# Values of an attention in four parts of the array, in two turns with two banks

## The chip, the cores and the metric

One core of a Trainium2 chip. The time is the device's microseconds for one execution of the whole program. The engines are TensorE (PE, its weight loads listed apart as PEld), VectorE (DVE), ScalarE (ACT), GpSimd (POOL) and SyncE (SP, which issues the loads). PE writes its results to PSUM, which has eight banks of 128 partitions x 512 floats.

## The reference

A sliding-window attention with sink tokens, and two feed-forward networks behind it, all in float32:

```python
# q, k, v: (2, 8, 768, 64), n_sink 4, window 128
scores = q @ k^T / 8
keep = (key < n_sink) | ((0 <= query - key) & (query - key < window))
a = softmax(where(keep, scores, -1e9))
x = (a @ v), heads side by side                # 1536 tokens x 512
x = ((x @ w_a) * (x @ w_b)) @ w_out            # d_ff 1536
out = square(max(x @ w_in, 0)) @ w_out2        # d_ff 2048
```

## The kernel before

The attention goes over 24 groups g of 128 queries and four heads: batch b = g // 12, block i of 128 tokens = (g % 12) // 2, half m of the heads. A query block sees its own block of keys, the block before it (for i > 0), and eight sink tokens. A group goes through these stages:

- `scores`: two pairs of heads pp, each with a PSUM tile of two banks, `scs[pp]`. Each matmul multiplies 64 rows (one head's 64 features, `half(keys, r)`) with 64 queries, so four of them use the four parts of the array: r picks the rows, z the columns. A float32 matmul is two records of the trace (L233). For i > 0 they are 200 or 208 columns wide, else 128.
- `soft0`, `soft1` (`maxima`, DVE L249 and L252): selection, mask and maximum, a pair at a time; `exp0`, `exp1` (ACT L260); `rec` (DVE L265, L266): sum and reciprocal.
- `sp` (POOL L289 to L291): the sinks' weights; `pst`, `st`: their transposition on PE (L321) and its copy by ACT (L327). `norm`, `normA`, `normP`: normalizing on DVE, ACT (L275) and POOL.
- `ptp` (PE L297): transposes the four heads' weights into one bank; `th` (ACT L301) copies that out; `lu` (POOL L312, L314) makes two masked copies, `lu[:, 0]` for the block itself (a key sees later queries) and `lu[:, 1]` for the block before (a key sees earlier queries).
- `x` (`values`, PE L335, L340): for each block j and head, a matmul of 128 keys x 64 features with 128 queries, two heads beside each other in the two column halves of the array; then two matmuls for the sinks, into the same bank. `xh` (ACT L348) and `xl` (DVE L351) split it into a rounded part and the rest.

Beside this runs `Beside`: `fill` issues the twelve matmuls (L660) of a piece of the first network's product into a bank of `psa`; `fu` (ACT L673) or `fm` (DVE L677) drains it in the next step. A fill may start when 512 tokens are attended: steps 11 to 26 have one each. `abs`, `ts`, `stt`, `stt2`, `cast`, `lo` decode weights (ACT L533, L549, DVE L537 to L551). `warm` issues small matmuls in the steps 0 to 4.

The order of the work on PE, DVE, ACT and POOL is written by hand: for each step g, `ORDER` names the stages in turn with a lag, so ("x", -3) is the x of group g - 3. Each engine takes its own instructions in that order; a wait on one stops all behind it. SP issues its loads by itself.

PSUM: four banks of scores; `bank()` hands out the rest in rotation for ptp, pst, x and warm, four banks until step 10 and two from then on, when two go to `psa`. Code that the change touches:

Of the kernel before, what the change touches and what calls it, by code (L numbers as in the profile page):

```python
# [10 lines left out]
F32 = mybir.dt.float32  # L11
# [19 lines left out]
    ("exp0", -1), ("exp1", -1), ("fm", 0), ("pst", -2), ("rec", -1), ("st", -2), ("fu", 0), ("scores", 0),  # L31
    ("x", -3), ("abs", 0), ("xh", -3), ("ptp", -2), ("th", -2), ("cast", -2), ("soft0", 0), ("soft1", 0), ("sp", -1),
# [3 lines left out]
WIDE = 10  # L36
# [113 lines left out]
def attention_fast(tc, ctx, c, cp, tp, q, k, v, vs_in, xh, xl, beside):  # L150
# [11 lines left out]
    banks = [ctx.enter_context(tc.tile_pool(name="ps_t", bufs=2, space=PSUM))]  # L162
    wide = ctx.enter_context(ExitStack())
    banks.append(wide.enter_context(tc.tile_pool(name="ps_u", bufs=2, space=PSUM, side="right")))
    turn = [0]

    def bank(name):

        turn[0] += 1
        return banks[turn[0] % len(banks)].tile([P, GH, P], F32, name=name, tag="tr")  # L170
# [49 lines left out]
    def scores(g):  # L220

        b, i, m = groups[g]
        n = b * NB + i
        for pp, sc in enumerate(scs):
            for r in range(2):
                row = half(keys, r)[:, 2 * m + pp].rearrange("d n s -> d (n s)")
                for z in range(2):
                    at, u0, u1 = PREV, i * SW, i * SW + P
                    if i > 0 and z == 0:
                        u0, u1 = u0 - SW, u0 + HK  # L230
                    elif i > 0:
                        at, u0, u1 = 0, u0 - PREV, u0 + SW
                    nc.tensor.matmul(sc[z * HK:(z + 1) * HK, r, at:at + u1 - u0],  # L233
                                     lhsT=half(queries[n], r)[:, 2 * m + pp, z * HK:(z + 1) * HK], rhs=row[:, u0:u1],
                                     start=True, stop=True)
# [93 lines left out]
    def values(g):  # L329

        b, i, m = groups[g]
        x = xs[g] = bank("x")[:, 0:2]
        for j, probs_t in enumerate(lus.pop(g)):
            for h in range(GH):
                nc.tensor.matmul(half(x, h % 2)[:, h // 2], lhsT=vals[g // 2 - j][:, GH * m + h], rhs=probs_t[:, h],  # L335
                                 start=j == 0 and h < 2, stop=False, skip_group_check=True)
        if i > 0:
            st = sts.pop(g)
            for pp in range(2):
                nc.tensor.matmul(x[:, pp], lhsT=vs[:, b, 2 * m + pp, :], rhs=st, start=False, stop=False,  # L340
                                 skip_group_check=True)
# [14 lines left out]
    def warm(n):  # L356
# [4 lines left out]
        for _ in range(n):  # L361
# [3 lines left out]
    stages = dict(scores=scores, ptp=probs, th=probs_copy, lu=probs_select, soft0=lambda g: maxima(g, 0),  # L365
                  soft1=lambda g: maxima(g, 1), exp0=lambda g: exps(g, 0), exp1=lambda g: exps(g, 1), rec=reciprocal,
                  sp=sinks, pst=sinks_turn, st=sinks_copy, x=values, xh=x_high, xl=x_low,
                  norm=normalize, normA=normalize_a, normP=normalize_p)
    warm(WARM0)
    for g in range(N + 3):  # L370
        if g == WIDE:
            banks.pop()
            wide.close()
            beside.open()
# [223 lines left out]
class Beside:  # L598
# [12 lines left out]
    def open(self):  # L611
        self.ps = self.stack.enter_context(self.tc.tile_pool(name="ps_a0", bufs=2, space=PSUM, side="right"))
# [29 lines left out]
class Ffn:  # L642
# [9 lines left out]
    def inner(self, ph, f, j, ts, ps_a):  # L652
# [3 lines left out]
        ps = ps_a.tile([P, ts.stop - ts.start], F32, name="psa", tag="z", bufs=2)  # L656
# [7 lines left out]
    def ahead(self, t0, last, beside, wk):  # L664
# [4 lines left out]
        for f in range(AHEAD1):  # L669
            u = wk.tile([P, T], F32, name="u", tag="u")  # L670
            pa = self.inner(0, f, 0, ts, beside.ps)
# [3 lines left out]
            pb = self.inner(0, f, 1, ts, beside.ps)  # L675
# [396 lines left out]
def sliding_window_moe_kernel(ctx, tc, q, k, v, vs, span, w_a, w_b, w_out, w_in2, w_out2, out):  # L1072
# [19 lines left out]
    def run(attend):  # L1092
# [3 lines left out]
        with ExitStack() as c0:  # L1096
# [3 lines left out]
            with ExitStack() as c1, tc.manual_schedule(engines=ORDERED):  # L1100
                attend(c1, beside)
            with tc.tile_pool(name="sb", bufs=1) as sb, tc.tile_pool(name="ks", bufs=NKEEP) as keep:
# [21 lines left out]
    def attend_any(ctx, beside):  # L1124
        attention_any(tc, c, q, k, v, xh, xl)
        beside.open()
# [74 lines left out]
```

## Time and profile before

| | |
|---|---|
| median of 3 runs | 627.29 us (625.4, 627.29, 627.45) |
| the profiled execution | 625.55 us, span 623.8 us |
| PE busy | 610.1 us, 98% of the span, 3302 matmul records |
| PEld, DVE, ACT, POOL busy | 79%, 77%, 50%, 9% |
| first fill | 46.97 us |
| x of the last group | 123.88 us |

The busy time of PE counts overlapping records once, and its ends are modelled. Times in the rows are us from the start of the span. A row of the order of time merges like instructions that follow each other (x16); in brackets stands how long the engine was idle before, and what released it.

### The profile page before, as it was taken

The numbers are of one execution on the slowest core, as the hardware profiler recorded it, in microseconds if no ns is written. First come the engines' busy times: TensorE is split into PE (matmuls) and PEld (weight loads), VectorE is DVE, ScalarE is ACT, GpSimd is POOL, SyncE is SP. The second block draws the span as 40 slices with busy tenths as digits, with TensorE's granted clock in tenths as the row PEclk, the third lists the DMA queues.
The fourth block names the chain that finished last, engine by engine and source line by source line (L and its number), as shares of the span: only waits on it lengthen the run. The fifth ranks groups of instructions, "written<-read, shape, count | busy, mean of one in ns | idle before, by whom it ended". The sixth has DMA issues, their size and how long they took to land.

```text
span 623.8 us, 9222 instructions
## 1 busy us (share of the span) xinstructions
PE 610.1 (98%) x3302; PEld 494.0 (79%) x3302; DVE 483.2 (77%) x1099; ACT 309.2 (50%) x706; POOL 56.5 (9%) x132
## 2 busy tenths in 40 slices
PE   9789999999999999999999999999999999999996
PEld 5557777888888888888888888888888888888884
DVE  7999998369999848959769999976797679834352
ACT  6998887525754424534433554563454345332220
POOL 2564255400000000000000000000000000000000
PEclk9999999999999999999999999999999999999999
DMA  8844423001223412202212013132032202000023
GB/s 273 260 117 151 153 69 102 2 34 55 82 92 112 126 43 101 69 34 68 101 35 101 1 34 102 69 108 95 34 102 68 68 34 68 0 2 2 0 100 108
DMA packets 22039, 49.51 MB, mean 79 GB/s; under 512 B 2080, under 2 KB 8736, under 8 KB 21984
## 3 DMA queue, kind: packets, MB, share of 16 engines
q1 hardware_dynamic: 21696, 48.70, 24.0%
q8 instruction: 28, 0.46, 0.3%
q14 instruction: 27, 0.22, 0.1%
q10 hardware_dynamic: 288, 0.13, 0.1%
HBM read 45.68 MB, written 3.15 MB: 78 GB/s over the span
## 4 chain that ended last, share of the span: by engine, by line


## 5 line engine op out<-in xcount | busy, mean ns | idle before, releaser
L660 PE MATMUL psa<-xh,wh 128*128 128x512 f32 x224 | 88.7, 396 | 0.0
L660 PE MATMUL psa<-xh,wl 128*128 128x512 f32 x224 | 87.5, 391 | 0.0
L660 PE MATMUL psa<-xl,wh 128*128 128x512 f32 x224 | 87.3, 390 | 0.0
L920 PE MATMUL acc<-wh,gh 128*128 128x512 f32 x192 | 74.8, 389 | 0.0
L920 PE MATMUL acc<-wh,gl 128*128 128x512 f32 x192 | 74.8, 389 | 0.0
L920 PE MATMUL acc<-wl,gh 128*128 128x512 f32 x192 | 74.7, 389 | 0.0
L551 DVE TENSOR_TENSOR wl<-wtmp,wh 128x512 fp32r<-128x512 f32 x68 | 47.3, 700 | 17.3 <-ACT wh L549 17.0
L549 ACT CAST wh<-wtmp 128x512 fp32r<-128x512 f32 x68 | 42.3, 622 | 37.0 <-PE acc L920 10.1
L67 ACT CAST gh<-ks 128x512 fp32r<-128x512 f32 x48 | 29.6, 621 | 52.5 <-PE acc L920 52.5
L533 ACT ACTIVATE wtmp<-wraw 128x512 f32<-128x512 f32 x68 | 45.7, 676 | 19.4 <-DVE wl L68 12.7
L920 PE MATMUL acc<-gl,wh 128*128 128x512 f32 x136 | 52.9, 389 | 0.0
L920 PE MATMUL acc<-gh,wl 128*128 128x512 f32 x136 | 52.9, 389 | 0.0
L920 PE MATMUL acc<-gh,wh 128*128 128x512 f32 x136 | 52.9, 389 | 0.0
L660 PEld LDWEIGHTS psa<-xh,wl 128*128 128x128 f32 x224 | 42.1, 188 | 9.0
L660 PEld LDWEIGHTS psa<-xl,wh 128*128 128x128 f32 x224 | 42.1, 188 | 8.3
L660 PEld LDWEIGHTS psa<-xh,wh 128*128 128x128 f32 x224 | 42.1, 188 | 8.2
L541 DVE SCALAR_TENSOR_TENSOR wtmp<-wraw,wtmp 128x512 int32<-128x512 int32 x68 | 47.0, 694 | 0.4
L544 DVE SCALAR_TENSOR_TENSOR wtmp<-wraw,wtmp 128x512 int32<-128x512 int32 x68 | 46.3, 684 | 0.7
L920 PEld LDWEIGHTS acc<-wh,gh 128*128 128x128 f32 x192 | 36.0, 188 | 7.5
L920 PEld LDWEIGHTS acc<-wh,gl 128*128 128x128 f32 x192 | 36.0, 188 | 7.5
L920 PEld LDWEIGHTS acc<-wl,gh 128*128 128x128 f32 x192 | 36.1, 188 | 7.4
L68 DVE TENSOR_TENSOR gl<-ks,gh 128x512 fp32r<-128x512 f32 x48 | 32.7, 686 | 10.3 <-ACT gh L67 9.9
(170 smaller groups left out, 1274.9 us busy)
## 6 DMA issues: line engine op xcount, KB each, us to landing
wraw<-in_moe_w_out_dram SPq DMA_DIRECT2D x28, 512.0 KB, 3.5
wraw<-in_moe_w_in_dram SPq DMA_DIRECT2D x16, 512.0 KB, 3.5
wraw<-in_moe_w_a_dram SPq DMA_DIRECT2D x12, 512.0 KB, 3.5
wraw<-in_moe_w_b_dram SPq DMA_DIRECT2D x12, 512.0 KB, 3.5
values<-in_v_dram SPq DMA_DIRECT2D x12, 256.0 KB, 4.3
keys<-in_k_dram SPq DMA_DIRECT2D x11, 272.0 KB, 4.8
queries<-in_q_dram SPq DMA_DIRECT2D x11, 256.0 KB, 3.8
out_dram<-part SPq DMA_DIRECT2D x11, 256.0 KB, 2.2
```

The source lines that it names most:

```text
L67: nc.scalar.copy(hi, src)
L68: return (lo_eng or nc.vector).tensor_sub(lo, src, hi.bitcast(F32))
L533: a = nc.scalar.activation(tf, up.bitcast(F32), AF.Abs)
L541: nc.vector.scalar_tensor_tensor(out=t, in0=up, scalar=0x3FFFFFFF, in1=t, op0=ALU.bitwise_or, op1=ALU.bitwise_and)
L544: nc.vector.scalar_tensor_tensor(out=t, in0=low, scalar=29, in1=t, op0=ALU.logical_shift_right, op1=ALU.bitwise_or)
L549: nc.scalar.copy(hi, tf)
L551: nc.vector.tensor_sub(lo, tf, hi.bitcast(F32))
L660: self.tc.nc.tensor.matmul(ps, lhsT=w[:, kt, :], rhs=x[:, kt, ts], start=n == 0, stop=n == 3 * KT - 1)
L920: nc.tensor.matmul(acc["ps"][d], lhsT=a, rhs=b, start=n == 0, stop=n == acc["total"] - 1)
```

## The change

The values run in four parts of the array as well: the keys of a block are cut into upper and lower 64 rows (r), and the two column halves stay for the two heads of a pair. [...] Where a half of the keys can only see half of the queries, the matmul has 64 columns instead of 128 (`part`). In the order, scores are cut into the two pairs, and it goes scores0, x0, scores1, x1, xs (the sinks' product).

The banks: four for scores, two for x with one buffer, one for ptp, pst and warm together, and one for the fills from the start; when the attention is over, the fills get two others.

```diff
--- before.py
+++ after.py
@@ -28,12 +28,11 @@
 NRAW, AHEAD = 3, 2
 
 ORDER = [
-    ("exp0", -1), ("exp1", -1), ("fm", 0), ("pst", -2), ("rec", -1), ("st", -2), ("fu", 0), ("scores", 0),
-    ("x", -3), ("abs", 0), ("xh", -3), ("ptp", -2), ("th", -2), ("cast", -2), ("soft0", 0), ("soft1", 0), ("sp", -1),
+    ("exp0", -1), ("exp1", -1), ("fm", 0), ("pst", -2), ("rec", -1), ("st", -2), ("fu", 0), ("scores0", 0),
+    ("x0", -3), ("scores1", 0), ("x1", -3), ("xs", -3), ("abs", 0), ("xh", -3), ("ptp", -2), ("th", -2), ("cast", -2), ("soft0", 0), ("soft1", 0), ("sp", -1),
     ("norm", -1), ("warm", 0), ("fill", 0), ("normA", -1), ("normP", -1), ("xl", -3), ("stt", -1),
     ("lo", -2), ("ts", 0), ("lu", -2), ("stt2", -1)]
 DECODE = [4, 8, 10, 11, 12, 13, 14, 15, 18, 19, 20]
-WIDE = 10
 VS = (3, 6)
 PINNED = 3
 WARM0 = 14
@@ -159,15 +158,12 @@
     p1 = ctx.enter_context(tc.tile_pool(name="at1", bufs=1))
     p2 = ctx.enter_context(tc.tile_pool(name="at2", bufs=2))
     ps_s = ctx.enter_context(tc.tile_pool(name="ps_s", bufs=1, space=PSUM))
-    banks = [ctx.enter_context(tc.tile_pool(name="ps_t", bufs=2, space=PSUM))]
-    wide = ctx.enter_context(ExitStack())
-    banks.append(wide.enter_context(tc.tile_pool(name="ps_u", bufs=2, space=PSUM, side="right")))
-    turn = [0]
+    ps_t = ctx.enter_context(tc.tile_pool(name="ps_t", bufs=1, space=PSUM))
+    ps_x = ctx.enter_context(tc.tile_pool(name="ps_x", bufs=1, space=PSUM))
+    beside.open(1)
 
     def bank(name):
-
-        turn[0] += 1
-        return banks[turn[0] % len(banks)].tile([P, GH, P], F32, name=name, tag="tr")
+        return ps_t.tile([P, GH, P], F32, name=name, tag="tr")
 
     pns, ths, sps, sts, lus, xs = ({} for _ in range(6))
 
@@ -217,11 +213,11 @@
     for sc in scs:
         nc.vector.memset(sc[:, :, 0:PREV + SW + HK], 0.0)
 
-    def scores(g):
+    def scores(g, pp):
 
         b, i, m = groups[g]
         n = b * NB + i
-        for pp, sc in enumerate(scs):
+        for sc in scs[pp:pp + 1]:
             for r in range(2):
                 row = half(keys, r)[:, 2 * m + pp].rearrange("d n s -> d (n s)")
                 for z in range(2):
@@ -326,18 +322,40 @@
         sts[g] = p2.tile([96, P], F32R, name="st", tag="st", bufs=NSP)
         nc.scalar.copy(sts[g], sps.pop((g, "t")))
 
-    def values(g):
+    mark = p1.tile([1, 1], F32, name="mark")
+    marks = []
+
+    def behind(later, earlier):
+        tc.add_manual_dep(later.ins, earlier.ins.name, mybir.DependencyInfo(
+            mybir.DependencyClass.Sync, mybir.DependencyReason.DATA), reason="rows change places")
+
+    def values(g, turn):
 
         b, i, m = groups[g]
-        x = xs[g] = bank("x")[:, 0:2]
-        for j, probs_t in enumerate(lus.pop(g)):
-            for h in range(GH):
-                nc.tensor.matmul(half(x, h % 2)[:, h // 2], lhsT=vals[g // 2 - j][:, GH * m + h], rhs=probs_t[:, h],
-                                 start=j == 0 and h < 2, stop=False, skip_group_check=True)
+        if turn == 0:
+            xs[g] = ps_x.tile([P, 2, 512], F32, name="x", tag="x")[:, :, 0:P]
+        x, lu = xs[g], lus[g]
+        part = {(0, 0): slice(0, P), (0, 1): slice(0, HK), (1, 0): slice(HK, P), (1, 1): slice(0, P)}
+        for n in range(len(lu)):
+            for r in range(2):
+                j, pp = (n ^ r if i > 0 else n), r ^ turn
+                for h in range(2 * pp, 2 * pp + 2):
+                    mm = nc.tensor.matmul(half(x, h % 2)[:, pp, part[r, j]], lhsT=half(vals[g // 2 - j], r)[:, GH * m + h],
+                                          rhs=half(lu[j], r)[:, h, part[r, j]], start=n == 0 and turn == 0, stop=False,
+                                          skip_group_check=True)
+                    if turn == 1 and n == 0:
+                        behind(mm, marks[0])
+        if turn == 0:
+            marks[:] = [nc.gpsimd.memset(mark, 0.0)]
+            behind(marks[0], mm)
+
+    def sinks_values(g):
+        b, i, m = groups[g]
+        lus.pop(g)
         if i > 0:
             st = sts.pop(g)
             for pp in range(2):
-                nc.tensor.matmul(x[:, pp], lhsT=vs[:, b, 2 * m + pp, :], rhs=st, start=False, stop=False,
+                nc.tensor.matmul(xs[g][:, pp], lhsT=vs[:, b, 2 * m + pp, :], rhs=st, start=False, stop=False,
                                  skip_group_check=True)
 
     def places(g):
@@ -362,16 +380,12 @@
             nc.tensor.matmul(ps, lhsT=beside.zero, rhs=beside.zero[:, 0:1].to_broadcast([P, 2 * P]), start=True,
                              stop=True)
 
-    stages = dict(scores=scores, ptp=probs, th=probs_copy, lu=probs_select, soft0=lambda g: maxima(g, 0),
+    stages = dict(scores0=lambda g: scores(g, 0), scores1=lambda g: scores(g, 1), ptp=probs, th=probs_copy, lu=probs_select, soft0=lambda g: maxima(g, 0),
                   soft1=lambda g: maxima(g, 1), exp0=lambda g: exps(g, 0), exp1=lambda g: exps(g, 1), rec=reciprocal,
-                  sp=sinks, pst=sinks_turn, st=sinks_copy, x=values, xh=x_high, xl=x_low,
+                  sp=sinks, pst=sinks_turn, st=sinks_copy, x0=lambda g: values(g, 0), x1=lambda g: values(g, 1), xs=sinks_values, xh=x_high, xl=x_low,
                   norm=normalize, normA=normalize_a, normP=normalize_p)
     warm(WARM0)
     for g in range(N + 3):
-        if g == WIDE:
-            banks.pop()
-            wide.close()
-            beside.open()
         if g % 2 == 0:
             load_kq(g // 2 + 2)
             load_v(g // 2 + 1)
@@ -608,8 +622,9 @@
         self.open_piece = None
         self.work = self.head()
 
-    def open(self):
-        self.ps = self.stack.enter_context(self.tc.tile_pool(name="ps_a0", bufs=2, space=PSUM, side="right"))
+    def open(self, n):
+        self.ps = self.stack.enter_context(self.tc.tile_pool(name=f"ps_a{n}", bufs=n, space=PSUM, side="right"))
+        self.tags = n
 
     def head(self):
         for t0 in range(0, self.NT, T):
@@ -649,11 +664,11 @@
         self.chores = []
         self.pace = 1
 
-    def inner(self, ph, f, j, ts, ps_a):
+    def inner(self, ph, f, j, ts, ps_a, bufs=2):
         W, xh, xl = self.W, self.xh, self.xl
         KT = xh.shape[1]
         hi, lo = (w.rearrange("p (k f) -> p k f", k=KT) for w in W.get(ph, f, j))
-        ps = ps_a.tile([P, ts.stop - ts.start], F32, name="psa", tag="z", bufs=2)
+        ps = ps_a.tile([P, ts.stop - ts.start], F32, name="psa", tag="z", bufs=bufs)
         n = 0
         for kt in range(KT):
             for w, x in ((hi, xh), (hi, xl), (lo, xh)):
@@ -668,11 +683,11 @@
         ts = slice(t0, t0 + T)
         for f in range(AHEAD1):
             u = wk.tile([P, T], F32, name="u", tag="u")
-            pa = self.inner(0, f, 0, ts, beside.ps)
+            pa = self.inner(0, f, 0, ts, beside.ps, beside.tags)
             yield "fu"
             nc.scalar.copy(u, pa)
             yield None
-            pb = self.inner(0, f, 1, ts, beside.ps)
+            pb = self.inner(0, f, 1, ts, beside.ps, beside.tags)
             yield "fm"
             nc.vector.tensor_mul(self.gs[t0 // T][:, f], u, pb)
             if last:
@@ -1099,6 +1114,7 @@
             beside = Beside(tc, W, F, wk0, c0, zero, NT)
             with ExitStack() as c1, tc.manual_schedule(engines=ORDERED):
                 attend(c1, beside)
+            beside.open(2)
             with tc.tile_pool(name="sb", bufs=1) as sb, tc.tile_pool(name="ks", bufs=NKEEP) as keep:
                 sx = slots(sb, NSUM)
                 F.sx = {(n, k): sx[3 * k + n - 2] for n in range(2, 5) for k in range(2)}
@@ -1123,7 +1139,6 @@
 
     def attend_any(ctx, beside):
         attention_any(tc, c, q, k, v, xh, xl)
-        beside.open()
 
     run(lambda ctx, beside: attention_fast(tc, ctx, c, cp, tp, q, k, v, vs, xh, xl, beside))
     slow = nc.values_load(c.slow[0:1, 0:1], min_val=0, max_val=1,
```

## Rows read from the trace of the kernel before

**Rows 1.** busy time by stretch: us, then busy us (records) of each engine, clock, DMA

```profile
30.00:40.00 10.00, 7.74 (x91) 4.60 (x89) 8.74 (x44) 8.80 (x33) 6.72 (x17) 1.00 0.49 130
...
50.00:60.00 10.00, 10.00 (x101) 8.14 (x101) 9.86 (x35) 8.25 (x27) 5.07 (x9) 1.00 0.44 132
```

**Rows 2.** order of time, PE alone, second regime: start, us, line, operation

```profile
49.98 0.67 PE L233 MATMUL sc<-keys,queries 64*64 64x128 f32 x16
50.58 1.09 PE L335 MATMUL x<-lu,values 128*64 128x128 f32 x16
...
60.49 0.93 PE L233 MATMUL sc<-keys,queries 64*64 64x200 f32 x16
61.35 1.09 PE L335 MATMUL x<-lu,values 128*64 128x128 f32 x16
62.38 0.44 PE L340 MATMUL x<-st,vs 96*128 96x128 f32 x2
```

**Rows 3.** instructions of tile x: duration ns min/median/max, first and last start

```profile
L335 PE MATMUL x<-lu,values x320: 272/273/325, 20.3 to 124.7; 128*64 128x128 f32 x160
```

**Rows 4.** busy time of PE in one very short stretch, records in flight in brackets

```profile
27.34:27.37 0.03, 0.03 (x5) 1.00 0.33 137
```

**Rows 5.** order of time: a small POOL memset, and POOL's answer to ACT

```profile
0.30 0.10 POOL L1141 MEMSET const-float32-0.0<- 128x1 f32 x1 [0.30 <-issue]
...
35.01 0.58 ACT L301 COPY th<-ptp 128x512 f32<-128x512 f32 x1
...
35.67 0.64 POOL L312 TENSOR_SCALAR_AFFINE_SELECT lu<-th 128x512 f32<-128x512 f32 x1 [0.36 <-ACT th L301]
```

**Rows 6.** order of time, all engines, around step 7 (first regime)

```profile
25.86 0.18 DVE L266 RECIPROCAL ss<-ss 128x4 f32<-128x4 f32 x1
...
26.22 0.24 POOL L289 TENSOR_TENSOR ex<-ex,ss 128x32 f32<-128x32 f32 x1 [1.74 <-PE ptp L297]
...
26.84 0.25 POOL L291 TENSOR_TENSOR sp<-ex,sp 128x32 fp32r<-128x32 f32 x1
...
27.15 0.27 PE L321 MATMUL pst<-identr,sp 128*96 128x128 f32 x1 [1.09 <-POOL sp L291]
...
28.23 0.63 POOL L314 TENSOR_SCALAR_AFFINE_SELECT lu<-th 128x512 f32<-128x512 f32 x1
...
28.27 0.41 DVE L351 TENSOR_TENSOR xl<-x,xh 128x256 fp32r<-128x256 f32 x1
...
28.51 1.09 PE L335 MATMUL x<-lu,values 128*64 128x128 f32 x16
...
29.53 0.44 PE L340 MATMUL x<-st,vs 96*128 96x128 f32 x2
...
30.01 0.37 ACT L348 CAST xh<-x 128x256 fp32r<-128x256 f32 x1
...
30.52 0.58 ACT L301 COPY th<-ptp 128x512 f32<-128x512 f32 x1
```

**Rows 7.** order of time: last exponential on ACT and DVE's sum, two steps

```profile
33.07 0.19 ACT L260 ACTIVATION_READ_ACCUMULATOR ex<-ex,nb 128x1 f32 x1
...
33.30 0.17 DVE L265 TENSOR_SCALAR ss<-ss 128x4 f32<-128x4 f32 x1
...
37.56 0.20 ACT L260 ACTIVATION_READ_ACCUMULATOR ex<-ex,nb 128x1 f32 x1
...
37.79 0.17 DVE L265 TENSOR_SCALAR ss<-ss 128x4 f32<-128x4 f32 x1 [0.43 <-ACT ex L260]
```

**Rows 8.** order of time: warm matmuls of step 2 and th

```profile
10.09 1.49 PE L362 MATMUL psw<-zero 128*128 128x256 bf16 x12
...
10.29 0.59 ACT L301 COPY th<-ptp 128x512 f32<-128x512 f32 x1 [0.21 <-PE ptp L297]
```

**Rows 9.** order of time: a fill's start and the drain of the one before

```profile
78.36 0.48 PE L660 MATMUL psa<-xh,wh 128*128 128x512 f32 x1
78.43 0.67 DVE L677 TENSOR_TENSOR gs<-u,psa 128x512 f32<-128x512 f32 x1
```

## The prediction

> **What bounds the kernel now.** I began with the busy time by stretch [rows 1]. The reader is to see two regimes inside the attention. From 30 to 40 us TensorE (PE) is busy 7.74 of 10 us and leaves gaps, while VectorE (DVE) and ScalarE (ACT) have 8.74 and 8.80; from about 47 us, when the first layer's matmuls ("fills") come into the steps, PE is busy without a gap, and so it stays (98% of the span as a whole). But DVE is then at 9.86 of 10, so PE is the bound by a hair only. The granted clock is 1.00 in both. Then I read PE's order of time in single steps of the second regime [rows 2], for the price of scores and of x. Third, the order of time of all engines in a step of the first regime [rows 6], to see who waits for x there. Fourth, the places where ACT and DVE meet [rows 7], and where the banks that the change takes away would be missed [rows 8, 9].
>
> **PE's work in a step, before.** Scores of 200 and 208 columns (mean 204) start at 60.49 and x at 61.35: 0.86 us; scores of 128 columns take 49.98 to 50.58: 0.60 [rows 2]. Sixteen records in four parts are four in a row for each part, so 4 x 76 columns cost 0.26: 0.855 ns for a column of a record. Four times 128 columns are then 0.44, and 0.16 is left for what happens once at a change of the array's shape (weights in, old work out). x: eight pairs of 128 columns, 8 x 0.109 = 0.875, and 0.16: 1.03, which is what 61.35 to 62.38 shows. Scores and x together: 1.89.
>
> **The same after.** A turn of the values is, in each part, two records of 128 and two of 64 columns: 0.219 + 0.109 = 0.328. Half of the scores is 2 x 204 columns: 0.349. Scores and values now have one shape, so 0.16 is paid once: 0.16 + 0.349 + 0.328 + 0.349 + 0.328 = 1.51, if the second turn never waits. That the four parts do run beside each other is seen in the scores: between 27.34 and 27.37 five matmuls are in flight, the turned sinks and four of scores, so four started within 0.03 us [rows 4].
>
> A bound from the other side: sixteen starts in the 0.44 of scores of 128 columns [rows 2] are the densest whole run of such records that a row shows. Were that the densest possible, a turn would be 0.44 and not 0.328, 0.22 more a step. I take 0.328, by the four starts.
>
> [...]
>
> **The wait between the turns.** The second turn waits for POOL's memset of the mark, which waits for the last matmul of the first turn. No row shows this pair of hops, so it is put together: a matmul of 128 columns lasts 0.273 [rows 3], of which 0.109 is streaming, so 0.16 lies behind the last column; POOL starts 0.07 after the th that it waits for (35.01 + 0.58 to 35.67) [rows 5], or 0.18 after DVE's reciprocal (25.86 + 0.18 to 26.22) [rows 6]; a small memset is 0.10 [rows 5]; from POOL's sp (26.84 + 0.25) to PE's pst 27.15 are 0.06 [rows 6]; weights in, 0.05 (a third of the 0.16). Sum 0.44 with the short response, which I take because the mark waits for one engine only, as th's reader does; 0.55 with the long one. POOL's own queue holds nothing ahead of the mark: the last thing before it is lu, which x needs anyway; behind it waits sp, for a reciprocal that comes later. The second half of the scores (0.349) covers most: 0.09 is left. A covered step is 1.60 against 1.89: 0.29 saved (0.18 with the long response). In the last three steps, 24 to 26, there are no scores to cover it: 0.16 + 0.328 + 0.44 + 0.328 = 1.26 against x alone at 1.03: 0.23 lost in each.
>
> **First regime: x comes later.** One x in place of a rotating bank means that the first turn waits for xl of the step before. It also needs both halves of lu at its start, since rows 64 to 127 read the other block first; before, the second half was needed only in mid-x. And the second half of the scores now stands behind this turn. In the step shown, xl ends at 28.68 and lu at 28.86, x started at 28.51 and st at 29.53 [rows 6]. After: the first turn at 28.91, then 0.05 + 0.328 + 0.44 + 0.328 + 0.11 = 1.26, st at 30.17: 0.64 late. ACT's xh (30.01) follows st directly, then th (30.52), then normalizing and the exponentials; the last of these ends at 33.26 and DVE's sum starts at 33.30; one step on, 37.76 and 37.79, after DVE stood idle for 0.43 [rows 7]. So in two steps the delay goes to DVE whole; in the other steps DVE has decoding to do before, and I take nothing. DVE is then 1.28, say 1.3, later. Bounds: 0, if earlier slack on ACT swallows it, and 7 x 0.64 = 4.5, if each of the seven such steps pays.
>
> The warm matmuls share the one bank with ptp, so in step 2 they wait for th (10.29 + 0.59 = 10.88) instead of starting at 10.09 [rows 8]: 0.84 with the hop, less the half of the scores and one change of shape that x no longer stands behind, 0.51: 0.3. DVE is not full there; I take 0, and keep 0.3 for the range. ptp and pst in one bank: pst waits for th of the step before, ptp for st's copy. Both copies are ACT's and end before the second regime's next use; in the first, x's own delay is longer. I take nothing.
>
> **Second regime: one bank for the fills.** A fill may now start only when the one before is drained. At 78.36 it starts while DVE's gs, which drains that bank, runs from 78.43 to 79.10 [rows 9]: 79.15, 0.80 late. As DVE is full until then, what PE saved before, it waits away here: at this fill PE is 0.80 behind the old time plus whatever DVE is late, 1.3: 2.1. After 80 us the decoding thins out (the last begins in step 20); I take DVE to drain in time from there, and PE counts again: six covered steps, 6 x 0.29 = 1.74 saved; three without scores, 0.69 lost. All else after the attention is PE's stream, unchanged. Sum: 2.1 - 1.74 + 0.69 = +1.05 us. Dropped parts: the sinks' product is only placed elsewhere, and the weight loads, twice as many, hide behind the other parts, as those of the scores do (they would cost up to 0.05 a turn).
>
> **The rivals.** (1) *Forecast*: DVE paces until 79 us and about 1 us is lost net: within 0.3% (1.9 us, about what a measurement of this kernel can tell from no change). Chance 0.60. (2) *PE's saving counts whole, faster*: DVE is not the pace, because its 9.86 hold enough air, or x comes no later in the first regime. Then ten covered steps from 47 us save 2.9 and three lose 0.69: -2.2, and up to 0.4 more where ACT gets x sooner: 624.7 to 625.1. For it: PE shows no waits in the second regime; against: the 0.80 of [rows 9]. 0.13. (3) *The round trip over POOL, slower*: if it takes 0.9 rather than 0.44, each of nine steps costs 0.46 more: +4.1, in all +5.2: 632.5. It decides from 0.55 on (nine times 0.1 takes +1.05 to the bound). For it: a response of 0.18 exists; against: 0.07 and 0.10 in [rows 5]. 0.10. (4) *More than two steps of the first regime pass the delay on, slower*: four of them, 2.6, make +2.3: 629.6; seven, +4.3: 631.5. 0.12. (5) *The change doesn't do what it says, slower*: upper and lower rows run one after the other; a turn is 0.66, nine steps lose 5.9: 634.2. By [rows 4] only 0.02. (6) *The starts are the limit, slower*: sixteen records never take less than 0.44, so nine steps lose 9 x 0.22 = 2.0 more: +3.1, 630.4. For it: no whole run in the rows is denser; against: [rows 4]. 0.03. [...]
>
> **How the numbers follow.** The profiled execution took 625.55 us (span 623.8); the median of the runs shown is 627.29, 1.74 above it. The forecast is put on the median: 627.29 + 1.05 = 628.3. Unknown costs alone give -1.1 (DVE not late, wait fully covered: 0.80 - 6 x 0.38 + 3 x 0.14) to +2.4 (DVE 1.6 late, long response), so 626.2 to 629.7; with the neighbours, rival 2 below and part of 4 above, 624.9 to 630.9. Faster 0.13; slower 0.10 + 0.12 + 0.02 + 0.03 = 0.27, of which 0.02 of rival 4 (three steps) stays under the bound: 0.25; same 0.60 + 0.02 = 0.62.
>
> **What would show it.** Right: x in the profile after as two groups some 0.33 long with about 0.09 of idle PE before the second; in the step near 28 us PE idle before x, released by lu or xl, and st 0.6 later; a PE gap before a fill near 79 us, released by gs; PE about 2 us behind there and catching up after. Wrong: fills that begin earlier than 46.97, or a second turn more than 0.2 late.

## The result, and the profile after

The changed kernel takes 634.67 us (median of 4, 631.96 to 636.14), the kernel before 626.52 beside it (median of 4, 625.4 to 627.45): ratio 1.0129, 95% interval 1.0097 to 1.016. It is slower by about 8 us, outside the range of the prediction (624.9 to 630.9).

The profiled execution took 631.96 us, with a span of 630.3. Three starts show where the time went. Step 2's scores start at 8.21 us (before 8.67; this varies by 0.9 from run to run, so lengths are counted from here). The first fill starts at 53.63 instead of 46.97. The last contiguous run of fills, behind the attention, starts at 131.38 instead of 125.18. So the stretch from the first fill to the last run became *shorter*, 77.75 against 78.21, and everything lost was lost before the first fill: 45.42 against 38.30 us from step 2.

The busy time by stretch of the changed kernel (us; busy us and records of PE, PEld, DVE, ACT, POOL; granted clock; DMA), where [rows 1] are those of before, and then finer:

```profile
20.00:30.00 10.00, 7.66 (x116) 5.68 (x119) 8.14 (x34) 5.90 (x24) 5.50 (x14) 0.78 0.66 196
30.00:40.00 10.00, 9.15 (x109) 7.20 (x109) 5.90 (x27) 6.94 (x27) 5.25 (x14) 0.53 0.20 57
50.00:60.00 10.00, 9.34 (x127) 7.29 (x128) 9.29 (x35) 9.01 (x31) 5.92 (x15) 1.00 0.54 145
...
22.00:24.00 2.00, 1.23 (x18) 0.95 (x15) 1.89 (x12) 1.43 (x4) 1.47 (x4) 1.00 0.58 154
24.00:26.00 2.00, 1.40 (x30) 0.91 (x28) 1.93 (x5) 1.84 (x10) 1.28 (x2) 0.91 0.54 143
26.00:28.00 2.00, 2.00 (x26) 1.71 (x22) 1.82 (x12) 0.03 (x1) 1.40 (x5) 0.50 0.39 117
...
38.00:40.00 2.00, 2.00 (x29) 1.62 (x22) 1.79 (x11) 0.85 (x2) 1.40 (x5) 0.67 0.00 0
```

The number behind the five busy times is the one to read: the clock. It is 0.91 from 24 to 26, 0.50 in each window from 26 to 38, 0.67 from 38 to 40, and 1.00 in every other window of 2 us up to 626. In windows of 0.2 us from 24 to 41 it is 1.00 or 0.50, but for the two in which it changes (0.63 from 25.60, 0.74 from 39.20). Read as mixtures of 1.00 and 0.50, the windows of 2 us make 0.36 + 12 + 1.32, some 13.7 us at half clock. PE is then "busier" (9.15 of 10 against 7.74 in [rows 1]) because its work takes longer, while DVE falls from 8.74 to 5.90. It waits for PE by way of ACT: from 26 to 40 us DVE waits 3.2 us for ACT's exponentials and ACT 4.6 us for x of PE, where the kernel before has 0.4 and 1.3.

In the first turn (`x0`) the upper rows work for pair 0 and the lower for pair 1, each pair in a bank of its own; in the second (`x1`) they change places, behind the mark. No run here has both row halves in one bank, so what that would do is not shown.

What PE did before and in the fall, in the order of time of PE alone (start, us, line, operation; in brackets the idle time before, and what released it):

```profile
10.60 1.16 PE L380 MATMUL psw<-zero 128*128 128x256 bf16 x9 [0.81 <-ACT th L297]
...
18.90 1.16 PE L380 MATMUL psw<-zero 128*128 128x256 bf16 x9 [0.67 <-ACT th L297]
...
23.68 0.24 PE L317 MATMUL pst<-identr,sp 128*96 128x128 f32 x1 [0.77 <-ACT th L297]
23.84 0.58 PE L229 MATMUL sc<-keys,queries 64*64 64x200 f32 x8
24.30 0.43 PE L343 MATMUL x<-lu,values 64*64 64x128 f32 x4
25.33 0.44 PE L343 MATMUL x<-lu,values 64*64 64x128 f32 x8 [0.60 <-POOL lu L310]
...
26.18 1.13 PE L343 MATMUL x<-lu,values 64*64 64x128 f32 x16
...
27.73 1.08 PE L293 MATMUL ptp<-identr,ex 128*128 128x128 f32 x4
29.63 0.31 PE L317 MATMUL pst<-identr,sp 128*96 128x128 f32 x1 [0.82 <-ACT th L297]
```

The warm matmuls, which answer to [rows 8] (the first row's view ends inside the twelve of step 2), and pst wait for th in the one transposes' bank, and the first turn (25.33) waits in its middle for the second half of lu. After that the second turn lasts 1.13 us and ptp 1.08; at full clock they last 0.56 and 0.63 (next fence). The longest single wait of PE ahead of this fall, from 9 us on, is the 0.81 above.

In the second regime the single steps came out near the prediction. A covered step, answering to [rows 2], and one of the last three, same view:

```profile
88.29 0.58 PE L229 MATMUL sc<-keys,queries 64*64 64x200 f32 x8
88.68 0.53 PE L343 MATMUL x<-lu,values 64*64 64x128 f32 x16
89.02 0.55 PE L229 MATMUL sc<-keys,queries 64*64 64x200 f32 x8
89.44 0.56 PE L343 MATMUL x<-lu,values 64*64 64x128 f32 x16
89.93 0.44 PE L358 MATMUL x<-st,vs 96*128 96x128 f32 x2
90.20 0.63 PE L293 MATMUL ptp<-identr,ex 128*128 128x128 f32 x4
...
119.93 0.56 PE L343 MATMUL x<-lu,values 64*64 64x128 f32 x16
120.73 0.56 PE L343 MATMUL x<-lu,values 64*64 64x128 f32 x16 [0.23 <-POOL mark L349]
121.22 0.44 PE L358 MATMUL x<-st,vs 96*128 96x128 f32 x2
```

From 88.29 to 89.93 are 1.64 us, against 1.89 before; sixteen records of a turn start within 0.34 (88.68 to 89.02). Without scores between the turns it is 1.29 (119.93 to 121.22) against 1.03. The fills' one bank, answering to [rows 9], shows in the order of time of DVE and PE:

```profile
73.78 0.68 DVE L692 TENSOR_TENSOR gs<-u,psa 128x512 f32<-128x512 f32 x1
...
74.52 0.50 PE L675 MATMUL psa<-xh,wh 128*128 128x512 f32 x1
```

The fill starts 0.06 after the gs that drains its bank. The fill of [rows 9], the seventh, waits so too; PE alone, in the changed kernel and then before:

```profile
84.48 0.63 PE L293 MATMUL ptp<-identr,ex 128*128 128x128 f32 x4
85.28 0.50 PE L675 MATMUL psa<-xh,wh 128*128 128x512 f32 x1 [0.17 <-DVE gs L692]
```

```profile
77.98 0.62 PE L297 MATMUL ptp<-identr,ex 128*128 128x128 f32 x4
```

It starts 0.80 behind the ptp ahead of it, where before it was 0.38 (77.98 to 78.36): some 0.4 late. The fill at 74.52, the fifth, is as late; no other is.

### The profile page after: what moved, and what is told of

Same layout as the page of the kernel before. It is cut to its first block, busy times and chain, and to the rows that moved or that the text cites. A ratio compares the mean times of both kernels' runs of the same rounds, so it can differ in the third digit from the quotient of the medians.

```text
span 630.3 us, 9940 instructions
## 1 busy us (share of the span) xinstructions
PE 611.6 (97%) x3654; PEld 498.0 (79%) x3654; DVE 483.0 (77%) x1099; ACT 309.0 (49%) x706; POOL 61.0 (10%) x156
## 4 chain that ended last, share of the span: by engine, by line
## 5 line engine op out<-in xcount | busy, mean ns | idle before, releaser
L555 DVE SCALAR_TENSOR_TENSOR wtmp<-wraw,wtmp 128x512 int32<-128x512 int32 x68 | 47.8, 708 | 0.4
L558 DVE SCALAR_TENSOR_TENSOR wtmp<-wraw,wtmp 128x512 int32<-128x512 int32 x68 | 47.2, 698 | 0.7
```

Of the source, the lines that this page charges most:

```text
L555: nc.vector.scalar_tensor_tensor(out=t, in0=up, scalar=0x3FFFFFFF, in1=t, op0=ALU.bitwise_or, op1=ALU.bitwise_and)
L558: nc.vector.scalar_tensor_tensor(out=t, in0=low, scalar=29, in1=t, op0=ALU.logical_shift_right, op1=ALU.bitwise_or)
```

## The experiments

Two theories came first. *Clock*: the changed kernel leaves PE idle more in steps 2 to 8, the granted clock falls there as the profile shows it (0.50), and that is the larger part of the loss. *Waits*: the longer way of x, the shared banks and the round trip over POOL cost all of it, and the clock costs nothing of its own, since PE is not full there. Within the first, it was open which idle time is to blame: the banks' or the turns'.

All runs, with medians of timed executions, the ratio to the kernel before on the same chip, and the three lengths of the profiled execution (first fill from the start of step 2's scores; first fill to last run of fills):

| run | us | ratio (95%) | to first fill | to last run |
|---|---|---|---|---|
| before | 625.6 to 626.5 | | 38.30 | 78.21 |
| after | 634.67 | 1.0129 (1.0097, 1.016) | 45.42 | 77.75 |
| e1_keep | 628.95 | 1.0056 (1.0038, 1.0075) | 42.31 | 77.97 |
| e2_warmbank | 633.76 | 1.0137 (1.0082, 1.0192) | 43.11 | 77.82 |
| e3_banks | 628.66 | 1.0045 (1.0031, 1.0058) | 39.99 | 79.09 |
| e4_twobanks | 631.85 | 1.0109 (1.0072, 1.0145) | 44.53 | 78.54 |
| e5_own_keep | 628.53 | 1.0039 (1.0024, 1.0054) | 42.07 | 77.97 |
| e7_fills2 | 627.54 | 1.0031 (1.0017, 1.0045) | 39.78 | 78.28 |
| e8_nowarm | 628.93 | 1.0054 (1.0037, 1.0071) | 40.29 | 78.24 |
| e10_banks_keep | 628.83 | 1.0041 (1.0026, 1.0055) | 40.53 | 79.08 |
| e12_hybrid | 626.01 | 1.0002 (0.9992, 1.0012) | 38.81 | 78.43 |
| e13_last | 624.92 | 0.9985 (0.9976, 0.9994) | 41.63 | 77.13 |
| e14_scores_first_keep | 630.12 | 1.0068 (1.0053, 1.0083) | 43.35 | 77.86 |
| e15_scores_first | 631.99 | 1.0104 (1.0089, 1.012) | 45.46 | 77.91 |
| e16_banks_warm | 626.95 | 1.0016 (1.0007, 1.0025) | 38.99 | 79.13 |
| e17_prev_first | 629.34 | 1.0049 (1.0032, 1.0066) | 41.48 | 78.97 |

The runs were spread over several chips, so the ratios compare better than the medians. Each length is that of one execution; those of after, e2, e4, e8, e13 and e15 hold a fall of the clock. The second length repeats well: e8_nowarm, which is the kernel before there, has 78.24 against 78.21. The first holds some 0.5 of scatter: as far as the first fill e12_hybrid is the kernel before, and yet it has 38.81 against 38.30. Its step 2 started 0.91 earlier, but the ptp of step 3 only 0.43, as PE's order of time shows for the kernel before and for e12_hybrid:

```profile
13.44 0.66 PE L297 MATMUL ptp<-identr,ex 128*128 128x128 f32 x4
```

```profile
13.01 0.66 PE L302 MATMUL ptp<-identr,ex 128*128 128x128 f32 x4
```

Counted from this ptp the two agree, with first fills at 46.97 and 46.57: 33.53 and 33.56. By this second count, which leaves step 2 out, e3_banks and e7_fills2 have 34.71, e16_banks_warm 34.03, e10_banks_keep 35.39, e17_prev_first 36.20, e5_own_keep 36.86, e1_keep 37.10 and after 40.21. Where it changes a reading, it stands beside it.

**Is it the clock?** e1_keep fills PE's idle time in steps 3 to 10 with small matmuls into the fills' bank, which is free then:

```diff
+KEEP = {3: 5, 4: 5, 5: 6, 6: 6, 7: 6, 8: 6, 9: 6, 10: 6}
...
+    def keep(n):
+        if n == 0:
+            return
+        ps = beside.ps.tile([P, T], F32, name="psk", tag="z", bufs=1)[:, 0:2 * P]
+        for _ in range(n):
+            nc.tensor.matmul(ps, lhsT=beside.zero, rhs=beside.zero[:, 0:1].to_broadcast([P, 2 * P]), start=True,
+                             stop=True)
...
                 warm(WARM.get(g, 0))
+                keep(KEEP.get(g, 0))
```

> The changed kernel with five or six small matmuls more at the end of each of steps 3 to 10, into the bank of the fills, which is free until step 11; they wait for nothing that the others don't. Theory A (the clock): in the changed kernel the granted clock was 0.50 from about 25.5 to 39 us, and that costs about 5 of its 8 us; kept busy, PE stays at 1.00, the first fill starts near 49 instead of 53.6, and the time is 628 to 630 (about 2 over the kernel before, for the waits). Theory B (the waits alone): the new waits for th, lu and xl cost all of it, the clock being a passenger: the time stays at 633 to 636 even at clock 1.00.

Its busy time by stretch:

```profile
20.00:30.00 10.00, 8.74 (x141) 6.15 (x138) 8.98 (x35) 6.97 (x27) 6.58 (x15) 1.00 0.60 188
30.00:40.00 10.00, 8.40 (x143) 5.91 (x143) 7.48 (x32) 8.85 (x37) 5.63 (x16) 1.00 0.29 82
```

With more work on PE the kernel is 5.7 us faster by the medians, 4.6 by the ratios: the clock stays at 1.00 in every window up to 135 us, and DVE has 7.48 instead of 5.90. The clock theory holds, though the first fill comes at 50.51 and not near 49. The waits are not all, but 3.4 us over the kernel before beside it remain.

**The banks alone.** e3_banks keeps the values and the order of the kernel before and takes the banks of the changed one:

```diff
-        x = xs[g] = bank("x")[:, 0:2]
+        x = xs[g] = ps_x.tile([P, 2, 512], F32, name="x", tag="x")[:, 0, 0:2 * P].rearrange("p (a t) -> p a t", a=2)
...
+    beside.open(1)
```

> The kernel before, its values and its order unchanged, with the banks of the changed one: one for ptp, pst and warm, one buffer for x, one bank for the fills. If the pinch of banks makes PE idle (theory A1), the clock falls here too and the time is 631 to 635. If the turns and their new order make it (theory A2), the clock stays at 1.00 and the time is 626.5 to 628.5.

The clock stayed at 1.00 in every window of the profiled execution up to 135 us. The banks cost 1.69 ahead of the first fill by the table (39.99 against 38.30) and 1.18 by the second count; before and e7_fills2, whose steps 2 both start at 8.67, differ by 1.48. Behind the first fill they cost 0.88 (79.09 against 78.21). So the banks alone don't lower the clock as it fell in the changed kernel.

e7_fills2 has two banks for the fills instead of one, e16_banks_warm the warm matmuls in the fills' bank; both are e3_banks else:

```diff
-    beside.open(1)
+    beside.open(2)
```

> The values and the order of the kernel before, with one bank for transposes and one for values, as in the changed kernel, but two banks for the fills from the start instead of one (the two row blocks of a value share a bank in either). Theory: the single bank of the fills is what lengthens the second stretch (first contiguous fill to the last group of fills 79.09 against 78.21): it comes back to about 78.2 to 78.4, the first regime stays at 48.2, and the time is 627.4 to 628.0. Rival: the single transposes' bank lengthens that stretch, and it stays at about 79.1, time 628.4 to 629.

```diff
-        ps = bank("psw").rearrange("p h t -> p (h t)")[:, 0:2 * P]
+        ps = beside.ps.tile([P, T], F32, name="psw", tag="z", bufs=1)[:, 0:2 * P]
```

> The values and the order of the kernel before on the changed kernel's banks, with the warm matmuls of steps 2 to 4 put into the fills' bank, which is free then, instead of the transposes' bank. Theory: the 1.2 us that the banks cost ahead of the first contiguous fill is the warm matmuls' wait for th in steps 2 to 4: the fill comes back to 46.9 to 47.4, the second stretch stays at 79.1, time 627.2 to 628.0 (628.66 without). Rival: it is pst's and ptp's waits for one another in one bank, or the one x: first fill 48.0 to 48.4, 628.4 to 629.

Both as the theories said (the second a little faster): the fills' bank is worth 0.81 of the second stretch (79.09 to 78.28), the warm matmuls' wait 1.00 of the first (39.99 to 38.99; 0.68 by the second count).

**Which idle time lowers the clock?** e4_twobanks gives the changed kernel a second transposes' bank until step 10 (the fills' bank opens then):

```diff
+    banks.append(wide.enter_context(tc.tile_pool(name="ps_u", bufs=1, space=PSUM, side="right")))
...
+        turn[0] += 1
+        return banks[turn[0] % len(banks)].tile([P, GH, P], F32, name=name, tag="tr")
```

> The changed kernel with a second bank for ptp, pst and warm until step 10, when it goes to the fills, which don't need it before. Theory A1 (the pinch of the transposes' bank idles PE and drops the clock): clock 1.00, first fill near 48.5, time 627 to 629.5. Theory A2 (the turns' own waits for lu and xl do it): the clock falls as before, 632 to 636.

e2_warmbank has its warm matmuls in the fills' bank, by the same two lines as e16_banks_warm.

> The changed kernel with the warm matmuls of steps 2 to 4 in the fills' bank, which is free then. On the old values this gave back 1.0 of the 1.7 us that the banks cost ahead of the first contiguous fill. Theory: the warm matmuls' wait is part of the idle time that lowers the clock, but the turns' waits in steps 5 to 8 are enough by themselves (as with the second transposes' bank): the clock still falls between 25 and 60 us, first fill 51 to 53, 629.5 to 632. Rival: without that wait the clock stays at 1.00: first fill about 48.5, 627 to 628.

e8_nowarm takes the warm matmuls of steps 2 to 4 from the kernel before:

```diff
-WARM = {0: 14, 1: 3, 2: 12, 3: 6, 4: 9}
+WARM = {0: 14, 1: 3, 2: 0, 3: 0, 4: 0}
```

> The kernel before without the warm matmuls of steps 2 to 4, otherwise unchanged: the price of a lower clock in this stretch without any new wait. Theory A: the clock falls to 0.50 in part of 10 to 47 us, and the time is 629 to 633. Theory B: a lower clock costs little there, since DVE paces: 626.5 to 628.

The busy time by stretch of e4_twobanks, e2_warmbank and e8_nowarm in turn:

```profile
30.00:40.00 10.00, 8.29 (x130) 5.65 (x130) 6.85 (x31) 8.29 (x35) 5.30 (x15) 0.83 0.27 82
40.00:50.00 10.00, 7.39 (x96) 5.14 (x90) 7.81 (x33) 6.50 (x25) 5.79 (x14) 0.83 0.46 136
```

```profile
30.00:40.00 10.00, 8.36 (x110) 6.47 (x110) 6.79 (x31) 7.33 (x30) 5.01 (x14) 0.66 0.28 82
```

```profile
10.00:20.00 10.00, 5.97 (x70) 3.34 (x74) 8.60 (x46) 9.18 (x34) 3.78 (x11) 0.93 1.07 362
20.00:30.00 10.00, 8.22 (x98) 5.28 (x90) 8.74 (x35) 6.94 (x27) 6.96 (x14) 0.90 0.65 197
```

The clock falls in all three. With the banks' waits eased, though not gone (e4, e2), the turns' waits are still enough; e2_warmbank's median lies above what was expected, as two of its four executions have mean clocks of 0.976 and 0.977, the others 0.991. Without any turn (e8) the idle time that the missing warm matmuls leave is enough: PE has 5.97 of 10 us from 10 to 20, where the kernel before has 8.86 at 1.00, and the time lies between what the two theories gave. So more idle time of PE goes with a lower clock without a turn too, and on the changed kernel's banks the turns make the difference: e3_banks, without them, kept 1.00 in its profile. Where the border lies, these runs don't settle: the other executions of e3_banks have mean clocks from 0.994 to 0.998, so in some of them the clock may have fallen as well; no trace shows it.

**What do the turns cost at full clock?** e10_banks_keep is the control, e3_banks with the small matmuls of e1_keep.

> A control: the values and the order of the kernel before, on the banks of the changed kernel, with the same small matmuls in steps 3 to 10 that held the clock in the changed kernel. Theory: those matmuls stand in TensorE's idle time and cost at most 0.3 us; the first contiguous fill comes at about 48.2 to 48.5, the time is 628.4 to 629.0, as without them (628.66), and what the changed kernel with them loses beyond this in the first regime (50.51 against 48.18) is the turns' own. Rival: the matmuls delay the heads' path by themselves: first fill past 49.0, time past 629.2; then part of what was put down to the turns is the matmuls'.

The theory asked for 0.3 at most; the small matmuls themselves cost 0.54 ahead of the first fill (40.53 against 39.99; 0.68 by the second count), which the medians don't show (628.83 against 628.66). The turns cost what e1_keep has beyond the control, 42.31 - 40.53 = 1.78 (1.71 by the second count), and behind the first fill they save 79.08 - 77.97 = 1.11.

For that 1.78 three edits were tried. e5_own_keep takes the own block first in both row halves, and e14_scores_first_keep puts both halves of the scores ahead of both turns up to step 12 (both are e1_keep else); e17_prev_first gives the control's old values the late start alone, with the earlier block first.

```diff
-                j, pp = (n ^ r if i > 0 else n), r ^ turn
+                j, pp = n, r ^ turn
```

> The changed kernel with the small matmuls in steps 3 to 10 that hold the clock, and with the order of blocks in a turn made the same for both row halves: the own block first, the earlier block second. The values and sums are the same. Theory A: the first turn is held up because its upper rows start with the earlier block, whose selected rows are ready at another time than the lower rows' own block, so the first turn waits for both selections; with the own block first in both, half of each turn goes earlier, the first contiguous fill comes about 50.0 (50.51 without this) and the time is 628.0 to 628.6. Rival: each turn needs both blocks before it ends, and the second turn can't start before the first's end, so nothing is won: first fill about 50.5, 628.7 to 629.3.

```diff
-    ("x0", -3), ("scores1", 0), ("x1", -3), ("xs", -3),
+    ("scores1", 0), ("x0", -3), ("x1", -3), ("xs", -3),
```

> The changed kernel with the small matmuls that hold the clock, and up to step 12 both halves of the scores ahead of the two turns instead of between them. Theory: in the first steps the first turn waits for lu's second half, and the second half of the scores queues behind it, so that DVE's maxima and ACT's exponentials come late; with the scores ahead the first contiguous fill comes at 49.0 to 49.6 (50.51 without), 627.6 to 628.3 us. Rival: x's own delay (lu, mark, the one x) sets the steps' pace; then the second turn, no longer covered, comes 0.2 later still: first fill 50.5 to 51.5, 628.9 to 630.

```diff
-        for j, probs_t in enumerate(lus.pop(g)):
+        for n, (j, probs_t) in enumerate(reversed(list(enumerate(lus.pop(g))))):
...
-                                 start=j == 0 and h < 2, stop=False, skip_group_check=True)
+                                 start=n == 0 and h < 2, stop=False, skip_group_check=True)
```

> The control (values and order of the kernel before on the changed kernel's banks, with the small matmuls) with the values of the earlier block ahead of those of the own block, so that x can't start before the second half of lu is there, as the first turn can't. The sum is the same. Theory: in the first regime x, xh, th, lu and the next x follow each other in a ring through PE, ACT and POOL that sets the step's length, and the later start lengthens it by 0.3 to 0.5 us in four steps or more: from step 2's scores to the first contiguous fill 42.0 to 43 us (40.53 in the control, 42.31 with the turns), 629.6 to 630.6. Rival: the late start is hidden, and it is the round trip over POOL or the mark's place that costs: 40.5 to 41, 628.6 to 629.2.

One step of PE's order of time in e1_keep, in the control and in e17_prev_first:

```profile
28.71 0.58 PE L230 MATMUL sc<-keys,queries 64*64 64x200 f32 x8
29.16 0.44 PE L344 MATMUL x<-lu,values 64*64 64x128 f32 x4
...
30.20 0.44 PE L344 MATMUL x<-lu,values 64*64 64x128 f32 x8 [0.60 <-POOL lu L311]
...
31.46 0.44 PE L359 MATMUL x<-st,vs 96*128 96x128 f32 x2
```

```profile
29.01 0.93 PE L231 MATMUL sc<-keys,queries 64*64 64x200 f32 x16
...
31.13 0.44 PE L338 MATMUL x<-st,vs 96*128 96x128 f32 x2
```

```profile
28.82 0.93 PE L231 MATMUL sc<-keys,queries 64*64 64x200 f32 x16
30.32 1.09 PE L333 MATMUL x<-lu,values 128*64 128x128 f32 x16 [0.57 <-POOL lu L312]
31.34 0.44 PE L338 MATMUL x<-st,vs 96*128 96x128 f32 x2
```

From the scores' start to the sinks' product that ends x: 2.75 with the turns, 2.12 in the control, 2.52 with the late start alone. So 0.40 of the 0.63 by which the turns make x later in this step come with the wait for lu's second half. Ahead of the first fill the late start alone costs 0.95 of the 1.78 (41.48 against 40.53; 0.81 of 1.71 by the second count), between what the two theories gave. That the scores queue behind the first turn is not it: with the scores ahead, the first fill came 1.04 *later* (43.35 against 42.31), and that theory falls. Own block first gave 0.24, and a time that can't be told from e1_keep's. The other half of the 1.78 is put down here to the round trip and the longer x in a ring (x, ptp on PE, th on ACT, lu on POOL, the next x), but no run took it by itself; it stays open.

e15_scores_first is the order of e14_scores_first_keep without the small matmuls:

> The same order (scores ahead of both turns up to step 12) in the changed kernel without the small matmuls. Theory: TensorE's idle time in steps 3 to 6 becomes less by what the scores no longer wait, but the warm matmuls and pst still wait for th, so the granted clock still falls somewhere between 20 and 45 us, for less time than the 13.7 us of the changed kernel: first fill 50 to 52.5, 629 to 632. Rival 1: the clock stays at 1.00, first fill about 48.5 to 49.5, 627.5 to 628.5. Rival 2: nothing changes: 53.6, 634.

The granted clock is 0.53 from 30 to 40 us, as in the changed kernel, and the first fill is no earlier: rival 2 as far as the profiled execution goes, though the median lies 2.7 us lower (1.6 by the ratios) and so at the end of what the theory gave.

**Is there a better version?** e12_hybrid keeps the values, order and banks of the kernel before up to step 12 and has the turns, with their banks, from there on (the fills have one bank throughout).

```diff
-        for name, lag in ORDER:
+        for name, lag in ORDER if g >= SWITCH else ORDER0:
```

> The values, order and banks of the kernel before up to step 12, and those of the changed kernel from step 12 (fills in one bank from step 10 on). Theory: the loss sits in the first steps alone, where nothing covers the turns; the first contiguous fill comes at about 47.0 as before, the granted clock stays 1.00 there, and the stretch to the last group of fills is 0.3 to 0.9 us shorter than before's 78.21: 624.6 to 625.6 us where the kernel before has 625.5. Rival: the single bank of the fills and the uncovered turns of the last steps cost as much as the covered steps save: 625.6 to 627.0.

e13_last besides takes the last three steps' values, which no scores cover, in one go:

```diff
+        if g >= N - 3:
+            for j in range(len(lu) if turn == 0 else 0):
+                for h in range(GH):
+                    nc.tensor.matmul(half(x, h % 2)[:, h // 2], lhsT=vals[g // 2 - j][:, GH * m + h], rhs=lu[j][:, h],
+                                     start=j == 0, stop=False, skip_group_check=True)
+            return
```

> The hybrid (values of the kernel before up to step 12, two turns from there), with the last three steps' values, which have no scores beside them, in one go with full rows as before; x keeps its two banks. Theory: an uncovered pair of turns takes 0.26 us more than x alone, so three steps give back 0.7 to 0.8: first contiguous fill to last group of fills 77.6 to 77.8 (78.43 in the hybrid), 625.0 to 625.4 us where the hybrid has 626.0. Rival: those steps hide the turns behind the fills' wait for their single bank, and nothing comes back: 78.3 to 78.5 and 625.8 to 626.2.

The hybrid went as its rival: equal to before. e13_last is faster than both kernels, than the kernel before by 0.15% (0.06 to 0.24), and 1.1 us below the hybrid by the medians, which is more than the 0.8 that three steps at 0.27 would give; no run accounts for the rest. One of its last steps, PE alone:

```profile
121.12 1.09 PE L350 MATMUL x<-lu,values 128*64 128x128 f32 x16
122.14 0.44 PE L373 MATMUL x<-st,vs 96*128 96x128 f32 x2
```

That is 1.02, where the changed kernel has 1.29. Its profiled execution took 627.78 us, 2.9 above the median, and its busy time by stretch shows why:

```profile
30.00:32.00 2.00, 0.77 (x9) 0.46 (x11) 1.75 (x10) 1.86 (x7) 1.10 (x4) 1.00 0.80 266
32.00:34.00 2.00, 1.94 (x26) 1.26 (x28) 1.87 (x9) 2.00 (x10) 1.53 (x4) 0.80 0.00 1
34.00:36.00 2.00, 2.00 (x16) 1.67 (x13) 1.66 (x12) 0.38 (x2) 1.19 (x4) 0.50 0.12 8
```

Up to step 10 this is the work of the kernel before, and yet the clock fell in this execution. The kernel before may stand near that border already: of its 21 executions beside this run, the three above 627 us have mean clocks of 0.995 and 0.996, the others 0.996 to 0.999.

## Why the prediction was wrong

**The step that failed** is the sentence "The granted clock is 1.00 in both". It is true of the trace before, and the sum took it for true of the kernel after. Yet the prediction itself had PE busy 7.74 of 10 us in the first regime [rows 1] and put new waits there, for th, lu, xl and the mark. It priced each as time on the path, or as nothing where other work hides it, and never asked what more idle time does to PE itself. Of the 45.42 - 38.30 = 7.12 us lost ahead of the first fill, the banks are 1.69, the turns at full clock 1.78, and the clock the rest, 3.65 (45.42 less 42.31, and the 0.54 that the small matmuls in 42.31 cost). By the second count 6.68 were lost: 1.18, 1.71 and 3.79. That is the profiled execution; others run to 636.14 us with a mean clock of 0.978, against 0.986 there. No rival had the clock in it.

**The banks in the first regime**, "I take nothing" with 0.3 kept for the warm matmuls, were mis-sized: 1.2 to 1.7. The wait for th is as described [rows 8], PE idle for 0.81 before the warm matmuls, but the prediction counted it in step 2 only; it comes in steps 2 to 4, and taking it away gives 0.7 to 1.0 back. "DVE is not full there" did not hide it.

**x later in the first regime** was right in kind and, within a step, in size: 0.63 (0.64 predicted from [rows 6]). What it passes on was put at two steps [rows 7], 1.3; it was 1.7 to 1.8, so more than two steps pay, the fourth rival's mechanism at a smaller size.

**The second regime** went by the mechanism predicted, and the sum came close partly by luck. A covered step takes 1.64 (1.60 predicted), an uncovered one 1.29 (1.26), so the round trip over POOL of 0.44, put together from [rows 3], [rows 5] and [rows 6], is borne out, and rivals 3, 5 and 6 fall: sixteen starts within 0.34 lie where [rows 4] put them (0.328), not at 0.44. The fills' single bank costs 0.88 by e3_banks (0.80 predicted); in the changed kernel the wait is not one fill that is 0.80 late, but two that are some 0.4 late each. Ahead of the fill of [rows 9] the savings were not all waited away: from the first fill it comes after 31.65 us, before after 31.39, so it is 0.26 late and not 0.80. Behind it the turns save less than predicted: 46.10 us to the last run of fills against 46.82, 0.72 where 1.74 - 0.69 = 1.05 was predicted, with 1.58 saved in the six covered steps and 0.86 lost in the last three. Together the stretch is 0.46 shorter, where 0.80 - 1.05 = -0.25 was predicted; the two misses partly cancel. Rival 2's saving exists, but the first regime takes it away many times over.

With the clock held, and 0.54 to 0.68 spent on holding it, the changed kernel takes 628.95 us, and the forecast was 628.3. That nearness is luck: the forecast stood on a median of 627.29 for the kernel before, and beside e1_keep that kernel takes 625.56. Against it the change costs 3.4 us at full clock, 2.7 to 2.9 without the small matmuls, where +1.05 was forecast; the banks and x in the first regime are what is missing. The clock, which the sum took for given, comes on top.

## What to carry to other kernels

Where TensorE is not full, ask of each new wait what it does to the granted clock as well as to the chain of waits: the lower clock cost more here (3.65) than the two other terms ahead of the first fill together (3.47), and small matmuls into a free bank, for 0.54 to 0.68, kept the clock at 1.00. Put a change only into the stage that gains by it: the turns pay where scores cover them, and there alone (e13_last) they win a little. A bank that looks idle in a busy stage may be what keeps an earlier stage closed up, as that of the warm matmuls did.

## What the runs showed of the hardware that was not expected

The longest wait does not decide whether the clock falls. e13_last keeps 1.00 through a window in which PE is busy 0.77 of 2 us and falls behind it, the kernel before has the same work at 1.00 throughout, with waits of 1.09 [rows 6] and, at 31.64, of 1.21, and the changed kernel falls after waits of 0.81 at most. PE's busy time doesn't tell them apart either: the kernel before has 6.99 of 10 us from 22 to 32, at 1.00, and the changed kernel 7.59 from 16 to 26, where it falls. Equal code can keep the clock in one execution and lose it in another. What does decide stays open. The two stretches, before and after:

```profile
22.00:32.00 10.00, 6.99 (x85) 4.40 (x87) 9.31 (x38) 9.12 (x35) 5.97 (x16) 1.00 0.66 193
```

```profile
16.00:26.00 10.00, 7.59 (x131) 5.38 (x133) 9.34 (x41) 8.42 (x36) 5.66 (x14) 0.98 0.85 269
```

POOL's lu and DVE's decoding took longer where they met. In the order of time of the changed kernel:

```profile
23.60 0.64 POOL L308 TENSOR_SCALAR_AFFINE_SELECT lu<-th 128x512 f32<-128x512 f32 x1 [0.38 <-ACT th L297]
...
23.96 0.83 DVE L555 SCALAR_TENSOR_TENSOR wtmp<-wraw,wtmp 128x512 int32<-128x512 int32 x1
24.19 1.08 POOL L310 TENSOR_SCALAR_AFFINE_SELECT lu<-th 128x512 f32<-128x512 f32 x1
...
24.82 1.00 DVE L558 SCALAR_TENSOR_TENSOR wtmp<-wraw,wtmp 128x512 int32<-128x512 int32 x1
```

lu takes 0.63 in [rows 6], and the medians of the two DVE lines over the whole span are 0.69 each. The last three rows take 1.86 us together (23.96 to 25.82); one after the other they would take 2.01. So most of lu's time is added to DVE's rather than hidden behind it, and the half of lu for which the first turn waits came 0.45 later. With the first row, all four take 2.22 us (23.60 to 25.82), where one after the other they would take 2.64, so 0.42 did overlap.
